# A fused attention and two-mixture kernel: the tile blocks of the first mixture reordered, ranks taken two slots behind the choice, and a fourth output row buffer

## The chip, the core and the metric

The kernel runs on one core of a Trainium2 chip. The metric is the device time of one execution in microseconds (us). Within the core TensorE (PE) multiplies matrices and leaves its results in PSUM banks; VectorE (DVE), ScalarE (ACT) and GpSimd (POOL) work on elements; SyncE (SP) issues most of the DMA transfers. Each engine works through its own list of instructions in order, and waits on semaphores for the others.

## The reference

2176 tokens of 512 numbers come out of a windowed attention with global tokens (4 sequences of 512 local and 32 global tokens, 8 heads). Two mixtures follow:

```python
h = x @ w_in                      # [2176, 512] @ [512, 2048]
g = where(h >= 1, h, where(h <= -1, 0, (h + 1)**2 / 4))
y = g @ w_out                     # [2176, 2048] @ [2048, 512]

logits = (y / |y|) @ (emb / |emb|).T / tau          # 8 experts
idx = argmax(logits, axis=1)
gate = softmax(logits)[arange, idx]
for e in range(8):
    m = idx == e
    out[m] = gate[m] * (relu(y[m] @ w1[e]) @ w2[e])  # 512 -> 1024 -> 512
```

## The kernel before

The tokens make 17 tiles of 128 rows: 16 of local tokens and one of all the global ones. Attention fills the first 155 us or so; the change doesn't touch it. Then one loop (L1361) writes out the order of the work slot by slot. There are 80 slots of the first mixture (5 blocks of tiles, 16 slices f of the 2048 inner columns each), then 40 of the second (5 blocks of its own, 8 slices each), and two more that finish it. A slot is counted below by its f in its block, or from 0 at the start of the second mixture.

In a slot of the first mixture TensorE runs `up1` (L759): twelve matmuls of 128 columns per tile, since each product is made of three with operands split into a high and a low part; the result `hps` has one of two PSUM banks. `act1` (L773) makes `g_` from it (two ScalarE passes `t_`, then VectorE), splits `g_` into `gh` (ScalarE) and later `gl` (`act1b`, L789, VectorE), and splits a slice of `w_out` into `woh` and `wol` (`wout`, L793). `down1` (L804) uses `gh` and `gl` two slots later: three matmuls of 512 columns for each tile, added up in one PSUM bank per tile over the 16 slices. So a block of four tiles has 24 matmuls a slot, and one of three has 12 shorter ones and 9. `sizes` (L623) gives the blocks 4, 2, 4, 4 and 3 tiles; the first two run interleaved, slice by slice. At a block's end `y_out` (L639) copies each tile's rows into a buffer `y` (three in rotation, and for the tiles in `YOB`, L637, one of the output row buffers `ob1` to `ob3`) and stores them to DRAM.

Then each tile must be routed: eight `logits` (L669, one VectorE pass of 512 columns per expert, against the expert's row held in `hTh`, `hTl`, `yTh`, `yTl`, `hb` or `ob0`), the sum of squares `ysq` (L652, ScalarE), `choose` (L677, five small VectorE instructions that end in the one-hot row `ohot`), and `route3` (L690), which ranks each token among those of its expert. `route3` has TensorE multiply `ohot` by a triangle and the running count `acc` by ones, in a PSUM bank of tag T (there are two); VectorE then adds `ohot` to `acc` (L701) and picks out the rank (L703, L707).

This work is spread over the slots of the next block as a list `rq`, one entry a slot, which is popped behind `act1` and ahead of `act1b` and `down1`. On VectorE an entry so stands between `wol` and `gl`, and on TensorE between the up and the down matmuls. `pieces` (L832) plans the list: each item has a cost (1.0 for a logit, 1.2 for `choose`, 0.8 for `route3`), `lim` is what a slot may take (3.5 with five tiles, 2.9 otherwise), and a `None` makes the rest of that tile wait for the next slot. The `None` behind `choose` puts `route3` one slot behind it. The last tiles' list (`pieces_end`, L864) is written out by hand, in six entries, and runs in slots 2 to 7 of the second mixture.

Other work has fixed places. In the third and fourth block x of the next block is loaded at f = 4 (`x_load`, L729) and split at f = 9 and 11 (`x_split`, L741: ScalarE copies the high part `xh`, VectorE subtracts for `xl`, in two pieces for the last block, whose last tile is the global one). At the end of the fourth block `pick` (L881) counts the tokens ranked so far and chooses the most frequent expert, whose weights are read from DRAM; the last block splits them (`es_split`, L1194: a ScalarE and a VectorE pass of 1024 columns each) and transposes the first tiles of the second mixture (`e_tr`, L1205: four matmuls into a bank of tag T, then two times `exh` on ScalarE and `exl` on VectorE). The second mixture multiplies all tiles by that expert (`e_up`, L1213, with `eg` and `el`; `e_down`, L1233), and stores the rows that chose it: `ob` (L1249) is written by VectorE or ScalarE, and an indirect store is issued by POOL. The rows of the other experts are gathered in groups of four lists of 32 (`Quad`, L1127): a gather, a transpose `qt`, matmuls `qo` with weights that SP loads by registers read from the routing result, and a `put` (L1115). `second` (L1266) hangs all this on slots with `hook`; `steps1` to `steps2`, `members`, `norms`, `gates`, `digits` and `gate_list` (L907 to L1045) are the small steps from ranks and logits to lists and gates.

Of the kernel before, what the change touches and what calls it, by code (L numbers as in the profile page):

```python
# [9 lines left out]
F32 = mybir.dt.float32  # L10
# [21 lines left out]
def kernel(  # L32
# [587 lines left out]


    MB = 4
    sizes = [4, 2, 4, 4, 3]  # L623
    esizes = [4, 4, 4, 3, 2]
    assert sum(sizes) == sum(esizes) == NTILE
    blocks = [(sum(sizes[:i]) * P, n) for i, n in enumerate(sizes)]
# [7 lines left out]
    rq = []  # L634


    YOB = {3: 1, 4: 2, 5: 3, 9: 1, 13: 1}  # L637

    def y_out(i, yp):  # L639
        if i in YOB:  # L640
# [11 lines left out]
    def ysq(i, y):  # L652
        jk = mp.tile([P, 2 * P], F32, name="jk", tag="jk")
        nc.scalar.activation(out=jk.bitcast(BF16), in_=y, func=AF.Square, accum_out=ssq[:, i : i + 1])
# [22 lines left out]
    def choose(i, n):  # L677

        ix = mp.tile([P, 3, 8], U32, name="ix", tag="ix")
        for j in range(n):  # L680
            nc.vector.max(out=mxl[:, i + j, :], in_=rawl[:, i + j, :])
            nc.vector.max_index(out=ix[:, j, :], in_max=mxl[:, i + j, :], in_values=rawl[:, i + j, :])
        ixf = mp.tile([P, 3], F32, name="ixf", tag="ixf")
        nc.vector.tensor_copy(out=ixf[:, :n], in_=ix[:, :n, 0])
        nc.vector.tensor_tensor(
            out=ohot[:, i : i + n, :], in0=iota[:, :E].unsqueeze(1).to_broadcast([P, n, E]),
            in1=ixf[:, :n].unsqueeze(2).to_broadcast([P, n, E]), op=ALU.is_equal,
        )
# [115 lines left out]
    def down1(g):  # L804
        bi, f = items[g]
        t0, nt = blocks[bi]
        B_ = bs[bi]
        if f == 0:
            B_.yp = [
                ps.tile([P, DM], F32, name=f"yp{i}", tag="T" if bi == 1 else "y", bufs=2 if bi == 1 else 4)  # L810
                for i in range(nt)
            ]
        (gh, gl, _), (woh, wol) = gq.pop(g), wq.pop(g)
        for i in range(nt):
            cs = slice(i * P, (i + 1) * P)
            for k, (gt, wt) in enumerate(((gh, woh), (gh, wol), (gl, woh))):
                nc.tensor.matmul(  # L817
                    B_.yp[i], lhsT=gt[:, cs], rhs=wt, start=f == 0 and k == 0, stop=f == KF - 1 and k == 2
                )
        if f == KF - 1:  # L820
            B_.y = [y_out(t0 // P + i, B_.yp[i]) for i in range(nt)]
            ty.extend((t0 // P + i, y) for i, y in enumerate(B_.y))
            n = (0, 5, 5, 4, 3)[bi]
            rq.extend({NB - 1: pieces_end}.get(bi, pieces)(*[ty.pop(0) for _ in range(n)]))

    ty = []
# [5 lines left out]
    def pieces(*ty):  # L832

        work = []
        for i, y in ty:
            work += [(1.0, lambda i=i, y=y, e=e: logits(i, y, e, e + 1)) for e in range(E)]
            work += [(0.0, lambda i=i, y=y: ysq(i, y)), (0.0, None)]
            work += [(1.2, lambda i=i: choose(i, 1)), (0.0, None), (0.8, lambda i=i: route3(i, 1))]


        lim = 3.5 if len(ty) == 5 else 2.9
        cost = 0.0
        heads = [list(work[13 * j : 13 * j + 13]) for j in range(len(ty))]
        slots = []
        wait = [0] * len(ty)
        while any(heads):
            now = []
            for j, h in enumerate(heads):
                if not h or wait[j] > len(slots):
                    continue  # L850
                while h and cost + h[0][0] <= lim * (len(slots) + 1) + 0.5:
                    c, f = h.pop(0)
                    if f is None:
                        wait[j] = len(slots) + 1
                        break
                    now.append(f)
                    cost += c
                if h and wait[j] <= len(slots):
                    break
            cost = max(cost, lim * len(slots))  # L860
            slots.append(lambda now=now: [f() for f in now])
        return slots

    def pieces_end(*ty):  # L864

        (ta, ya), (tb, yb), (td, yd) = ty
        return [
            lambda: (logits(ta, ya, 0, 5), ysq(ta, ya)),
            lambda: (logits(ta, ya, 5, 8), choose(ta, 1), logits(tb, yb, 0, 2)),
            lambda: (logits(tb, yb, 2, 7), ysq(tb, yb)),  # L870
            lambda: (route3(ta, 1), logits(tb, yb, 7, 8), choose(tb, 1), logits(td, yd, 0, 3), ysq(td, yd)),
            lambda: (logits(td, yd, 3, 8), choose(td, 1)),
            lambda: (route3(tb, 1), count(route3(td, 1)), steps1()),
        ]


# [356 lines left out]
    def e_down(q, tiles=None):  # L1233
        b, f = divmod(q, KF2)
        t0, nt = eblocks[b][0] // P, eblocks[b][1]
        B_ = eb[b]
        if f == 0:
            B_.yp = [ps.tile([P, DM], F32, name=f"eo{i}", tag="y", bufs=4) for i in range(nt)]
        gh, gl = eq[q]
        wh, wl = [w[:, (f % 2) * DM : (f % 2 + 1) * DM] for w in wA[KD + f // 2]]  # L1240
        for i in range(nt) if tiles is None else tiles:
            cs = slice(i * P, (i + 1) * P)
            for k, (a, w) in enumerate(((gh, wh), (gh, wl), (gl, wh))):
                nc.tensor.matmul(  # L1244
                    B_.yp[i], lhsT=a[:, cs], rhs=w, start=f == 0 and k == 0, stop=f == KF2 - 1 and k == 2
                )
            if f == KF2 - 1:
                t = t0 + i
                ob = rp.tile([P, DM], F32, name="ob", tag=f"ob{1 + t % 3}")  # L1249
                if i % 2:  # L1250
                    nc.scalar.activation(out=ob, in_=B_.yp[i], func=AF.Copy, scale=gt[:, 1, t : t + 1])
                else:
                    nc.vector.tensor_scalar(  # L1253
                        out=ob, in0=B_.yp[i], scalar1=gt[:, 1, t : t + 1], scalar2=None, op0=ALU.mult
                    )
                nc.gpsimd.indirect_dma_start(  # L1256
                    out=outs[t], out_offset=bass.IndirectOffsetOnAxis(ap=ide[:, t : t + 1], axis=0), in_=ob,
                    in_offset=None, bounds_check=NTOK - 1, oob_is_err=False,
                )
# [3 lines left out]
    def hook(q, *fs):  # L1263
        hooks.setdefault(q, []).extend(fs)

    def second():  # L1266

        for c in range(6, NC):
            hook(c - 6, lambda c=c: es_split(c))
        for b in range(1, NEB):  # L1270
            q, nt = KF2 * (b - 1), eblocks[b][1]
            if b > 1:
                hook(q + 1, lambda b=b: e_load(b, 0), lambda b=b: e_load(b, 1))
                q += 3
            for i in range(nt):
                hook(q + i, lambda b=b, i=i: e_tr(b, i))
                if i + 2 < nt:
                    hook(q + i, lambda b=b, i=i: e_load(b, i + 2))
        TE = blocks[NB - 2][0] // P
        hook(-11, lambda: norms(0, TE))  # L1280
        hook(-7, lambda: gates(0, TE))
        hook(-5, lambda: members(0, TE))
        hook(7, steps_e)
        hook(8, steps_e2, lambda: members(TE, NTILE), steps1b)
        hook(9, steps1c, lambda: quads[0].regs(0, NQ4))
        hook(10, steps2, lambda: norms(TE, NTILE))
        quads = [Quad(j) for j in range(NS1)]
        hook(11, quads[0].gather)
        hook(12, lambda: gates(TE, NTILE))
        hook(13, quads[0].trans)  # L1290
        hook(13, lambda: R.update(rl=digits(R["ohhi"], NTILE, NSTEP, gb)))
        hook(14, lambda: R.update(gsl=gate_list(R["rl"])))
        hook(25, lambda: R.update(nst=nc.values_load(R["exi"][0:1, 0, NQ:], min_val=0, max_val=NQ)))
        for n in range(0, NS1 * NSUB, 2):
            (j, s), q = divmod(n, NSUB), 14 + 3 * n // 4
            r = quads[j]
            hook(q - 3, lambda r=r, s=s: (r.load(s), r.load(s + 1)))
            hook(q, lambda r=r, s=s: (r.mm(s), r.mm(s + 1)))
            if s in (KD, 2 * KD):
                hook(q, lambda r=r, s=s: r.htr(s // KD - 1))  # L1300
            if s == KD and j + 1 < NS1:
                hook(q, lambda j=j: quads[j + 1].regs(0, NQ4))
            if s == 2 * KD and j + 1 < NS1:
                hook(q, lambda j=j: quads[j + 1].gather())
            if s == NSUB - 4 and j + 1 < NS1:
                hook(q, lambda j=j: quads[j + 1].trans())
            if s == NSUB - 2:
                hook(q, lambda r=r: r.put())
# [164 lines left out]
```

## Time and profile before

| | |
|---|---|
| Median of 3 runs (lowest, highest) | 778.2 us (777.36, 779.43) |
| The profiled execution, and its span | 777.95 us, 776.2 us |
| Mean granted clock of TensorE | 0.992 of full |
| TensorE, VectorE, ScalarE, GpSimd busy | 96%, 62%, 48%, 18% of the span |

The profile is one execution as recorded on the chip. The span runs from its first to its last instruction, and the profiled execution's own time is 1.75 us longer. Busy time is given for the whole span and for stretches of it; the granted clock is a share of TensorE's full speed. A wait is the idle time of an engine ahead of an instruction, put down to whatever was last to release it. A timeline row gives the start, the length, the engine, the line, the operation, what is written and read, how many instructions are merged in the row, and in brackets the idle time ahead of it with its releaser. Successive VectorE instructions overlap a little, so their starts are closer than their lengths.

### The profile page before, as it was taken

How to read it: one execution, taken by the hardware profiler on the slowest of the kernel's cores; microseconds unless marked ns; L12 is line 12 of the kernel's file. 1: busy time of each engine (PE TensorE's matmuls, PEld its weight loads, DVE VectorE, ACT ScalarE, POOL GpSimd, SP SyncE). 2: the span in 40 equal slices, each digit the busy share in tenths (PEclk: the TensorE clock that was granted, in tenths of full speed). 3: DMA queues.
4: the chain of work that ended last, by engine and by line, in shares of the span. 5: the costliest groups of instructions: out<-in, count | busy, mean ns of one | idle time of the engine just before them, and what ended most of it. 6: DMA issues, size and time to landing. Idle time of an engine off the chain costs nothing.

```text
span 776.2 us, 14130 instructions
## 1 busy us (share of the span) xinstructions
PE 741.5 (96%) x4861; PEld 596.4 (77%) x4861; DVE 484.0 (62%) x1475; ACT 373.0 (48%) x930; POOL 142.1 (18%) x301
## 2 busy tenths in 40 slices
PE   6999898899999999999999999979999999999996
PEld 5777676788888888888888888868878866677765
DVE  5688888487887757777576867887866402211111
ACT  4888888655455565464545555555311212112110
POOL 5676676402111100000000010000004002002011
PEclk9999999999999999999999999999999999999999
DMA  8588886323233522000200004203201777546340
GB/s 186 130 233 232 242 248 148 110 80 108 87 132 113 184 88 82 1 1 0 82 1 0 1 1 161 83 28 106 71 0 69 244 242 285 183 141 215 109 149 25
DMA packets 74653, 89.36 MB, mean 115 GB/s; under 512 B 27488, under 2 KB 45920, under 8 KB 74576
## 3 DMA queue, kind: packets, MB, share of 16 engines
q1 hardware_dynamic: 64176, 78.96, 33.6%
q10 hardware_dynamic: 8720, 4.46, 2.0%
q0 software_dynamic: 1680, 4.98, 1.6%
q8 instruction: 40, 0.66, 0.3%
q14 instruction: 37, 0.30, 0.1%
HBM read 79.77 MB, written 13.65 MB: 120 GB/s over the span
## 4 chain that ended last, share of the span: by engine, by line
issue 62%; PE 6%; DVE 5%; DMA 3%; POOL 2%; ACT 2%; POOLq 0%; ACTq 0%; DVEq 0%
PE hps L768 3%; DMA out<-ob,ide 2%; PE yp L817 2%; POOL out L1256 1%; DVE wf L221 1%; DVE wf L218 1%; DVE wol L801 1%; DVE wf L215 0%; DMA raw<-in_moe_w_in 0%; POOL gt L959 0%; DVE wof L218 0%; PE pv L534 0%; POOL yg L1110 0%; PE pv L545 0%; DVE wof L221 0%
## 5 line engine op out<-in xcount | busy, mean ns | idle before, releaser
L768 PE MATMUL hps<-xh,winh 128*128 128x512 f32 (+2 forms) x320 | 115.2, 360 | 1.7 <-DVE g__2920 L784 1.7
L768 PE MATMUL hps<-xh,winl 128*128 128x512 f32 (+2 forms) x320 | 114.5, 358 | 0.0
L768 PE MATMUL hps<-xl,winh 128*128 128x512 f32 (+2 forms) x320 | 114.4, 358 | 0.0
L817 PE MATMUL yp<-woh,gh 128*128 128x512 f32 x272 | 108.0, 397 | 0.0
L817 PE MATMUL yp<-wol,gh 128*128 128x512 f32 x272 | 106.7, 392 | 0.0
L1228 DVE SCALAR_TENSOR_TENSOR el<-eh,eg 128x512 fp32r<-128x512 f32 (+2 forms) x40 | 24.5, 612 | 117.7 <-ACT eg L1227 117.4
L1227 ACT ACTIVATE eg<-eh 128x512 fp32r<-128x512 f32 (+2 forms) x40 | 21.4, 535 | 99.7 <-PE eh L1222 87.5
L768 PEld LDWEIGHTS hps<-xh,winh 128*128 128x128 f32 x320 | 60.5, 189 | 10.5 <-DVE g__2920 L784 1.9
L768 PEld LDWEIGHTS hps<-xh,winl 128*128 128x128 f32 x320 | 60.4, 189 | 8.5
L768 PEld LDWEIGHTS hps<-xl,winh 128*128 128x128 f32 x320 | 60.4, 189 | 7.5
L1256 POOL DMA_INDIRECT out<-ob,ide x17 | 18.2, 1073 | 230.0 <-DVE ob L1253 224.4
L1222 PE MATMUL eh<-exh,wh 128*128 128x512 f32 (+2 forms) x160 | 59.8, 374 | 0.0
L471 ACT ACTIVATE sm<-sm,st 128x160 f32<-128x160 f32 x128 | 53.4, 425 | 12.5 <-DVE st L461 12.1
L817 PEld LDWEIGHTS yp<-wol,gh 128*128 128x128 f32 x272 | 51.4, 189 | 9.5
L817 PEld LDWEIGHTS yp<-woh,gh 128*128 128x128 f32 x272 | 51.3, 188 | 9.4
L1222 PE MATMUL eh<-exh,wl 128*128 128x512 f32 (+2 forms) x160 | 57.3, 358 | 0.9 <-PEq L1427 0.9
L1222 PE MATMUL eh<-exl,wh 128*128 128x512 f32 (+2 forms) x160 | 57.3, 358 | 0.0
L493 POOL TENSOR_SCALAR pn<-sm,st 128x128 f32<-128x128 f32 x128 | 51.0, 417 | 23.6 <-DVE kw L339 7.0
L1244 PE MATMUL eo<-wh,eg 128*128 128x512 f32 x136 | 53.3, 392 | 0.0
L1244 PE MATMUL eo<-wl,eg 128*128 128x512 f32 x136 | 53.2, 391 | 0.0
L1244 PE MATMUL eo<-wh,el 128*128 128x512 f32 x136 | 53.1, 391 | 0.0
L801 DVE TENSOR_TENSOR wol<-wof,woh 128x512 fp32r<-128x512 f32 x64 | 43.9, 686 | 0.0
(797 smaller groups left out, 1598.0 us busy)
## 6 DMA issues: line engine op xcount, KB each, us to landing
rw<-in_moe_w SPq DMA_DIRECT2D x128, 256.0 KB
raw<-in_moe_w_out SPq DMA_DIRECT2D x12, 512.0 KB
raw<-in_moe_w_in SPq DMA_DIRECT2D x11, 512.0 KB
k<-in_k_l SPq DMA_DIRECT2D x16, 256.0 KB
xsc<-xs ACTq DMA_DIRECT2D x16, 256.0 KB
ysc<-y SPq DMA_DIRECT2D x16, 256.0 KB
rw<-in_moe_w SPq DMA_DIRECT2D x8, 512.0 KB
ye<-ysc SPq DMA_DIRECT2D x16, 256.0 KB
```

The costliest lines, as they stand in the source:

```text
L218: nc.vector.scalar_tensor_tensor(out=du, in0=hi, scalar=0xC0000000, in1=du, op0=ALU.bitwise_and, op1=ALU.bitwise_or)
L221: nc.vector.scalar_tensor_tensor(out=du, in0=lo, scalar=29, in1=du, op0=ALU.logical_shift_right, op1=ALU.bitwise_or)
L471: nc.scalar.activation(out=sm[:, i, :], in_=sm[:, i, :], func=AF.Exp, scale=-1.0, bias=st[:, 0, i : i + 1], accum_out=st[:, 1, i : i + 1],)
L493: eng_of[AT["f4"][i]].tensor_scalar(out=pn[:, i, :].rearrange("p (c x) -> p c x", c=2), in0=sel(sm[:, i, :]), scalar1=st[:, 2, i : i + 1], ...
L768: nc.tensor.matmul(hp_[:, :n], lhsT=wt[:, kk, fs], rhs=xt, start=kk == 0 and i == 0, stop=kk == KD - 1 and i == 2)
L801: nc.vector.tensor_tensor(out=wol, in0=wof[f // 2][:, f % 2, :], in1=woh.bitcast(F32), op=ALU.subtract)
L817: nc.tensor.matmul(B_.yp[i], lhsT=gt[:, cs], rhs=wt, start=f == 0 and k == 0, stop=f == KF - 1 and k == 2)
L1222: nc.tensor.matmul(hps[:, :n], lhsT=w[:, fs], rhs=x, start=kk == 0 and i == 0, stop=kk == KD - 1 and i == 2)
L1227: nc.scalar.activation(out=gh, in_=hps[:, :n], func=AF.Relu)
L1228: nc.vector.scalar_tensor_tensor(out=gl, in0=hps[:, :n], scalar=0.0, in1=gh.bitcast(F32), op0=ALU.max, op1=ALU.subtract)
L1244: nc.tensor.matmul(B_.yp[i], lhsT=a[:, cs], rhs=w, start=f == 0 and k == 0, stop=f == KF2 - 1 and k == 2)
L1256: nc.gpsimd.indirect_dma_start(out=outs[t], out_offset=bass.IndirectOffsetOnAxis(ap=ide[:, t : t + 1], axis=0), in_=ob, in_offset=None, bo ...
```

## The change

The blocks become 4, 2, 4, 3 and 4 tiles. A second `None` puts `route3` two slots behind `choose`; the rates become 3.7 with five tiles and 2.3 otherwise. The last block's four tiles have a list of seven entries, in which the last two tiles are ranked by one call of `route3`. The hooks of the second mixture that depend on the routing, and all of the quads, move by one slot. `ob` gets a fourth buffer, `yTl`, and tile 16 in place of tile 13 has its y in `ob1`.

```diff
-    sizes = [4, 2, 4, 4, 3]
+    sizes = [4, 2, 4, 3, 4]
...
-    YOB = {3: 1, 4: 2, 5: 3, 9: 1, 13: 1}
+    YOB = {3: 1, 4: 2, 5: 3, 9: 1, 16: 1}
...
-            n = (0, 5, 5, 4, 3)[bi]
+            n = (0, 5, 5, 3, 4)[bi]
...
-            work += [(1.2, lambda i=i: choose(i, 1)), (0.0, None), (0.8, lambda i=i: route3(i, 1))]
-
-
-        lim = 3.5 if len(ty) == 5 else 2.9
+            work += [(1.2, lambda i=i: choose(i, 1)), (0.0, None), (0.0, None), (0.8, lambda i=i: route3(i, 1))]
+
+
+        lim = 3.7 if len(ty) == 5 else 2.3
         cost = 0.0
-        heads = [list(work[13 * j : 13 * j + 13]) for j in range(len(ty))]
+        heads = [list(work[14 * j : 14 * j + 14]) for j in range(len(ty))]
...
-        (ta, ya), (tb, yb), (td, yd) = ty
+        (ta, ya), (tb, yb), (tc_, yc), (td, yd) = ty
         return [
-            lambda: (logits(ta, ya, 0, 5), ysq(ta, ya)),
-            lambda: (logits(ta, ya, 5, 8), choose(ta, 1), logits(tb, yb, 0, 2)),
-            lambda: (logits(tb, yb, 2, 7), ysq(tb, yb)),
-            lambda: (route3(ta, 1), logits(tb, yb, 7, 8), choose(tb, 1), logits(td, yd, 0, 3), ysq(td, yd)),
-            lambda: (logits(td, yd, 3, 8), choose(td, 1)),
-            lambda: (route3(tb, 1), count(route3(td, 1)), steps1()),
+            lambda: (logits(ta, ya, 0, 6), ysq(ta, ya)),
+            lambda: (logits(ta, ya, 6, 8), choose(ta, 1), logits(tb, yb, 0, 4), ysq(tb, yb)),
+            lambda: (logits(tb, yb, 4, 8), choose(tb, 1), logits(tc_, yc, 0, 1)),
+            lambda: (route3(ta, 1), logits(tc_, yc, 1, 6), ysq(tc_, yc)),
+            lambda: (route3(tb, 1), logits(tc_, yc, 6, 8), choose(tc_, 1), logits(td, yd, 0, 3)),
+            lambda: (logits(td, yd, 3, 8), choose(td, 1), ysq(td, yd)),
+            lambda: (count(route3(tc_, 2)), steps1()),
         ]
...
-                ob = rp.tile([P, DM], F32, name="ob", tag=f"ob{1 + t % 3}")
+                ob = rp.tile([P, DM], F32, name="ob", tag=("ob1", "ob2", "ob3", "yTl")[t % 4])
...
-        hook(7, steps_e)
-        hook(8, steps_e2, lambda: members(TE, NTILE), steps1b)
-        hook(9, steps1c, lambda: quads[0].regs(0, NQ4))
-        hook(10, steps2, lambda: norms(TE, NTILE))
+        hook(8, steps_e)
+        hook(9, steps_e2, lambda: members(TE, NTILE), steps1b)
+        hook(10, steps1c, lambda: quads[0].regs(0, NQ4))
+        hook(11, steps2, lambda: norms(TE, NTILE))
         quads = [Quad(j) for j in range(NS1)]
-        hook(11, quads[0].gather)
-        hook(12, lambda: gates(TE, NTILE))
-        hook(13, quads[0].trans)
-        hook(13, lambda: R.update(rl=digits(R["ohhi"], NTILE, NSTEP, gb)))
-        hook(14, lambda: R.update(gsl=gate_list(R["rl"])))
-        hook(25, lambda: R.update(nst=nc.values_load(R["exi"][0:1, 0, NQ:], min_val=0, max_val=NQ)))
+        hook(12, quads[0].gather)
+        hook(13, lambda: gates(TE, NTILE))
+        hook(14, quads[0].trans)
+        hook(14, lambda: R.update(rl=digits(R["ohhi"], NTILE, NSTEP, gb)))
+        hook(15, lambda: R.update(gsl=gate_list(R["rl"])))
+        hook(26, lambda: R.update(nst=nc.values_load(R["exi"][0:1, 0, NQ:], min_val=0, max_val=NQ)))
         for n in range(0, NS1 * NSUB, 2):
-            (j, s), q = divmod(n, NSUB), 14 + 3 * n // 4
+            (j, s), q = divmod(n, NSUB), 15 + 3 * n // 4
             r = quads[j]
             hook(q - 3, lambda r=r, s=s: (r.load(s), r.load(s + 1)))
```

## Rows read from the trace of the kernel before

In the tables of stretches the columns are the length, the busy time (with the number of instructions) of PE, PEld (weight loads), DVE, ACT and POOL, the granted clock, the DMA engines' busy share and GB/s.

**Rows 1.** Page, part 1: busy us (share of the span) x instructions.
```profile
PE 741.5 (96%) x4861; PEld 596.4 (77%) x4861; DVE 484.0 (62%) x1475; ACT 373.0 (48%) x930; POOL 142.1 (18%) x301
```

**Rows 2.** Table of stretches: length, then busy us (x instructions) of each engine, granted clock.
```profile
320.00:340.00 20.00, 20.00 (x93) 16.38 (x92) 13.69 (x36) 10.71 (x19) 0.00 (x0) 1.00 0.00 0
...
500.00:520.00 20.00, 15.39 (x85) 13.51 (x83) 17.79 (x59) 11.00 (x23) 0.00 (x0) 1.00 0.18 53
```

**Rows 3.** TensorE's waits from 150 us: us in total, times, longest.
```profile
PE rk L696 <- DVE ohot L685: 4.7, 2, 4.2
...
PE rk L697 <- DVE acc L701: 1.4, 1, 1.4
...
PE qo L1178 <- DVE gsl L991: 1.4, 1, 1.4
```

**Rows 4.** Table of stretches of 2 us, columns as in rows 2.
```profile
520.00:522.00 2.00, 1.95 (x10) 1.59 (x11) 2.00 (x6) 0.00 (x0) 0.00 (x0) 0.72 0.00 0
522.00:524.00 2.00, 2.00 (x7) 1.61 (x6) 0.95 (x3) 1.89 (x4) 0.00 (x0) 0.50 0.00 0
524.00:526.00 2.00, 2.00 (x13) 2.00 (x12) 1.97 (x8) 1.47 (x2) 0.00 (x0) 0.93 0.04 10
```

**Rows 5.** Timeline of VectorE, last block: start, us, instruction.
```profile
516.14 1.22 DVE L1095 TENSOR_TENSOR wl<-rw,wh 128x1024 fp32r<-128x1024 f32 x1
...
519.17 0.17 DVE L681 MAX8 mxl<-rawl 128x8 f32<-128x8 f32 x1
...
519.91 0.69 DVE L672 SCALAR_TENSOR_TENSOR jk<-y,ebchTh 128x512 bf16<-128x512 f32 x1
```

**Rows 6.** Timeline of VectorE, one slot of three tiles.
```profile
472.55 0.56 DVE L784 SCALAR_TENSOR_TENSOR g__5998<-t__5997,hps 128x384 f32<-128x384 f32 x1 [0.67 <-ACT t__5997 L783]
...
473.67 0.69 DVE L672 SCALAR_TENSOR_TENSOR jk<-y,ebchTl 128x512 bf16<-128x512 f32 x1
...
475.50 0.56 DVE L791 TENSOR_TENSOR gl__6000<-g__5998,gh 128x384 fp32r<-128x384 f32 x1
...
476.74 0.56 DVE L784 SCALAR_TENSOR_TENSOR g__6045<-t__6044,hps 128x384 f32<-128x384 f32 x1 [0.68 <-ACT t__6044 L783]
```

**Rows 7.** Timeline of VectorE, fourth block (four tiles).
```profile
398.29 0.69 DVE L784 SCALAR_TENSOR_TENSOR g__5268<-t__5267,hps 128x512 f32<-128x512 f32 x1 [0.97 <-ACT t__5267 L783]
...
403.73 0.69 DVE L784 SCALAR_TENSOR_TENSOR g__5316<-t__5315,hps 128x512 f32<-128x512 f32 x1 [1.58 <-ACT t__5315 L783]
```

**Rows 8.** Timeline of VectorE, split of the next block's x.
```profile
422.41 0.69 DVE L755 TENSOR_TENSOR xl<-xl,xh 128x512 fp32r<-128x512 f32 x1 [0.61 <-ACT xh L753]
```

**Rows 9.** Timeline, last block: VectorE's `gl__6304`, and TensorE's first use of it.
```profile
503.21 0.56 DVE L791 TENSOR_TENSOR gl__6304<-g__6302,gh 128x384 fp32r<-128x384 f32 x1
...
507.37 0.40 PE L817 MATMUL yp<-woh,gl__6304 128*128 128x512 f32 x1
```

**Rows 10.** Timeline, second mixture: VectorE and TensorE about the last two ranks.
```profile
574.98 0.69 DVE L1228 SCALAR_TENSOR_TENSOR el<-eh,eg 128x512 fp32r<-128x512 f32 x1 [0.82 <-ACT eg L1227]
...
575.59 0.15 DVE L701 TENSOR_TENSOR acc<-acc,ohot 128x8 bf16<-128x8 bf16 x1
...
575.79 0.19 PE L697 MATMUL rk<-acc,ones_bf 128*128 128x8 bf16 x2 [1.40 <-DVE acc L701]
...
576.05 0.17 DVE L703 TENSOR_TENSOR rt<-rk,ohot 128x8 f32<-128x8 f32 x1
```

**Rows 11.** Timeline, second mixture: VectorE's second `exl`, TensorE's first quad matmul.
```profile
621.41 0.42 DVE L1106 TENSOR_TENSOR exl<-tt,exh 128x256 fp32r<-128x256 f32 x1 [0.44 <-ACT exh L1105]
...
621.98 1.92 PE L1178 MATMUL qo<-rw,yTh 128*32 128x512 f32 x16 [1.39 <-DVE gsl L991]
```

**Rows 12.** Who waited for tile `ob` (us, times); then POOL's timeline.
```profile
  ACT ob L1251: 9.3, 2
...
759.56 0.98 POOL L1119 DMA_INDIRECT out<-ob,ids  x1 [12.28 <-DVE ob L1118]
...
771.92 0.98 POOL L1256 DMA_INDIRECT out<-ob,ide  x1 [0.31 <-ACT ob L1251]
```

## The prediction

> **What bounds the kernel now.** I began with the busy table of the page: TensorE is busy 96% of the span [rows 1]. Then the table of stretches of 20 us, to see where it is not full: from 160 us to the tail nearly every one has 20.00 us of TensorE work, as 320 to 340 has, and 500 to 520 has 15.39 [rows 2]. TensorE sets the pace, so what counts is why it stands still. Its list of waits from 150 us on gives three that the change touches [rows 3]: 4.7 us for `ohot`, one of them 4.2; 1.4 for `acc`; 1.4 put down to `gsl`. The 4.2 us cost more than themselves: right after them, in the stretches of 2 us from 520, the granted clock is 0.72, 0.50 (the lower of its two levels, 1.2 GHz) and 0.93 [rows 4], which loses (0.28 + 0.50 + 0.07) x 2 = 1.7 us.
>
> Why the 4.2: `choose` of the third tile began on VectorE at 519.17, and its rank matmuls, one slot behind it in TensorE's order, had been due some 4 us earlier [rows 5]. A slot of three tiles takes 4.19 us (472.55 to 476.74, `g__` to `g__`), and VectorE is at work for 3.5 of it with three logits [rows 6]. The last block adds splits of weights (1.22 each [rows 5]) and transposed tiles to that, so VectorE falls behind and the rank waits for it.
>
> **The change, part by part.** The sum is made against the profiled execution: 777.95 us, which is a span of 776.2 and 1.75 around it, and 0.25 under the median of 778.2.
>
> *Blocks of 3 and 4 tiles exchanged.* The same matmuls run in another order, so TensorE's own work stays. The choice of the expert still comes after the ranks of tiles 0 to 8 (the planner has the last of them in slot 14 of the fourth block, before and after) and TE stays 10, so the second mixture has the same expert and the same work. What moves is VectorE's load. The last block now has slots of 5.44 us [rows 7]; in 16 of them, 87 us, VectorE has 16 x 1.83 (`g_`, `wol`, `gl` at 0.61 from start to start), 24 logits x 0.61, three choices and ranks x 1.2, six splits x 1.2 and four transposed tiles x 1.3 (two `exl` of 0.42 with 0.44 between them [rows 11]): 29.3 + 14.6 + 3.6 + 7.2 + 5.2 = 60, and the small instructions of gates and members. No lag is left there.
>
> *The fourth block, now of three tiles, becomes the tight place.* Its slots have 1.60 us of `g_`, `wol` and `gl` (1.12 for the first two, 0.56 less an overlap of 0.08), logits at 0.61 (1.83 for three) [rows 6], a choice at 0.74 (519.17 to 519.91) [rows 5] and a rank at 0.46 (575.59 to 576.05) [rows 10]. Working the planner through by hand at the rate of 3.7 gives for slots 2 to 15: 4.04, 3.43, 4.04, 4.17, 3.43, 4.02, 4.04, 5.99, 3.56, 6.14, 4.02, 3.43, 3.89, 2.34, or 56.5 us against 14 x 4.19 = 58.7. Slots 9 and 11 hold the split of the next block's x: before, 0.61 us of waiting for ScalarE and 0.69 for the columns of two tiles [rows 8]; for three tiles, and 0.42 for the shared one, I take 2.1. VectorE's lag is then 1.8 us after slot 9, 3.1 after 11, 3.0 after 12, 2.2 after 13. How much is free: in the block of three tiles before, `gl__6304` ended at 503.77 and TensorE first used it at 507.37 [rows 9]; of these 3.6 us 0.5 (the shorter wait for `ohot`) and 0.2 (four transposes, 512 columns in all, at 5.44 / 24 per matmul of 512) won't be there, so 2.9, and 2.4 where a slot has four logits instead of two and a choice. The ranks, two slots behind, have a slot more. A lag of 3.1 meets 2.4 to 2.9: I put a stall of 0.5 us there; its ends are 0 and 6 (rival a).
>
> *Ranks two slots behind.* No instruction is added; the extra slot of each list is paid by the rates, and the last rank still comes in the slot where it came before. Removed: 4.7 us of waits and 1.7 of clock [rows 3, 4].
>
> *Seven steps at the end, ranks of the last two tiles in one group.* One more tile's logits, choice and rank move into the second mixture, with slots of about 5.4 us. The fullest of them (six logits, a choice, `el`, a transposed tile) asks 3.7 + 0.7 + 0.6 + 1.3 = 6.3, the next 4.4, so a lag of 1 us is gone one slot later, ahead of any rank that needs it. The group has the eight matmuls of two single ranks, and one product, one reduction and one sum less. Before, the second rank waited 1.40 us for `acc`, whose sum stood behind `el` on VectorE [rows 10]; in the group TensorE adds the first tile's counts itself, and that wait is gone. The last choice stays one slot ahead of its rank, as before, where no wait is listed [rows 3]. Against grouping speaks the Trainium skill, Perfetto Trace Analysis, section Optimizing Scalar/DVE Operations: where VectorE isn't saturated but leaves bubbles on other engines, instructions should be broken up so that work is done sooner. VectorE was idle 0.82 us ahead of that `el` [rows 10]; by the page the group would win nothing, and the sum would be 1.4 smaller. I go by the row, since the wait is for a sum that the group does away with.
>
> *Everything behind it one slot later.* This passes POOL's norms and gather, SP's register and weight loads and TensorE's quads, all by the same slot, so the distances between them stay; the loads of transposed tiles, which stand behind the register loads on SP, keep their slots. The last `put`'s store, issued at 759.56, moves by a slot; the kernel's last one goes at 771.92 [rows 12], so it stays inside. One distance changes. In slot 14 a transposed tile, the gate list and the first quad matmul stood together, and TensorE stood 1.39 us ahead of the quad, until 621.98 [rows 11]. The row names `gsl`, the last thing to end; but there are two banks for such tiles, the gate list had taken one, and the quad got the other, which the transposed tile's second `exl` left only at 621.83. Now that tile is a slot ahead. Removed: 1.4 us (0 if the wait was for `gsl`, which stays where it was).
>
> *A fourth output buffer.* ScalarE waited 9.3 us in two places for a store to land before it could write `ob` [rows 12]; TensorE's waits show none of it [rows 3], being fed two slots ahead. I take 0. `yTl` is last read in slot 7 and first written as `ob` in slot 9. The y tiles 13 and 16 only exchange buffers that are free long before.
>
> **Sum:** 4.7 + 1.7 + 1.4 + 1.4 = 9.2 removed, 0.5 added, 8.7 less: 769.25 for the profiled execution, 769.5 for the median. The ends: 9.2 less and a little of ScalarE's 9.3, about 767, and rival (a)'s 775.
>
> **Rivals.**
> (a) *VectorE becomes the bound of the fourth block.* It is filled to 56.5 of 58.7 us. Behind a late ScalarE copy it lost 0.61 us [rows 8]; lost in each of 14 slots that makes 8.5 more, 6.3 over the supply and 3.8 over what is free: a stall of 4 to 6 us, 773 to 775. For it: slots 9 and 11 ask 6 us each. Against it: with 3.5 us of work a slot of three tiles still left it 0.68 idle [rows 6]. The Trainium skill, Perfetto Trace Analysis, section Identifying the Most-Contended Engine, speaks for it: it judges TensorE by its weight loads and VectorE by occupancy, which from 500 to 520 are 13.5 and 17.8 us [rows 2], so that by the page VectorE bounds such a block. By the waits it held TensorE up at ranks alone. Chance 0.2.
> (b) *The wait only moves.* A slot more doesn't cure the last block's lag; waits for `gl` take the place of those for `ohot`, and only the 2.8 us in the second mixture are won: 775.4. Against it: 60 of 87 us. Chance 0.08.
> (c) *Slower.* In the two slots with the x split VectorE is held so long by ScalarE's copies, which stand behind `gh` and `ysq`, that TensorE stalls 4.2 us twice and loses 1.7 us of clock each time: 11.8 against 9.2, 780.8. It decides once that stage costs VectorE some 13 us more than tallied, and these copies were waited for 0.61 us [rows 8]. Chance 0.05.
> (d) *No change:* stalls of about 9 us in all stay or return elsewhere, 777 to 779. Chance 0.07.
>
> **The numbers.** The forecast has 0.6, and 767 to 771.5 for itself. 0.3%, 2.3 us, is about what a measurement of this kernel can tell from no change: faster than 775.9 takes the forecast, (a) and (b), 0.88; within it (d), 0.07; slower (c), 0.05. The range, 766.9 to 775.5, takes in (a), (b) and the ends.
>
> **What would show it.** Right: no wait for `ohot` above 0.3 us, none for `acc` or `gsl`; a granted clock of 1.00 from 160 us to the tail; VectorE nearly full in the fourth block, with at most 1 us of waits for `gl` in its slots 11 to 14; no ScalarE wait for a store ahead of `ob`. Wrong: TensorE waits of over 2 us or a clock under 1.00 in the fourth block, or a new wait of quads or gathers in the second mixture.

## The result, and the profile after

The changed kernel takes 769.78 us (median of four runs, 767.39 to 771.02) beside 778.5 for the kernel before on the same chip: a ratio of 0.9885, 95% interval 0.9856 to 0.9914. The forecast was 769.5. The profiled execution took 769.06 us, of which 767.4 are its span.

The page's busy table first, then the table of stretches of the fourth block (360 to 440 us, now of three tiles) and the last one, with the columns of [rows 2]:

```profile
PE 741.1 (97%) x4861; PEld 596.6 (78%) x4861; DVE 483.1 (63%) x1472; ACT 372.3 (49%) x930; POOL 139.9 (18%) x301
```

```profile
380.00:400.00 20.00, 20.00 (x102) 18.11 (x101) 18.13 (x50) 11.52 (x23) 0.00 (x0) 1.00 0.21 68
400.00:420.00 20.00, 20.00 (x107) 17.71 (x106) 17.94 (x58) 12.10 (x25) 0.00 (x0) 1.00 0.00 0
420.00:440.00 20.00, 20.00 (x107) 17.41 (x106) 17.61 (x54) 11.13 (x24) 2.10 (x1) 1.00 0.01 1
...
500.00:520.00 20.00, 20.00 (x95) 16.39 (x94) 16.79 (x41) 12.51 (x23) 0.00 (x0) 1.00 0.20 66
```

TensorE's busy time is what it was [rows 1]; the 500 to 520 that had 15.39 us of it [rows 2] has 20.00, at a clock of 1.00. VectorE is now fullest in the fourth block, 17.6 to 18.1 of 20. TensorE's waits from 150 us to the tail are these two, both there before (1.7 and 0.9 us):

```profile
PE hps L768 <- DVE g__2920 L784: 1.7, 1, 1.7
PE eh L1223 <- PEq L1428: 0.7, 1, 0.7
```

All three of [rows 3] are gone. To see where the time came from I cut each profiled execution at two marks: the first up matmul, and the last down matmul of the first mixture. In the view of a tile these are the first start of `hps` (148.1 us before, 149.2 after) and the last start of `yp`; this is the latter's row of the changed kernel:

```profile
L817 PE MATMUL yp<-wol,gh x272: 387/389/401, 159.8 to 536.5; 128*128 128x512 f32 x136
```

| us | ahead of the first mixture | first mixture | from there to the end |
|---|---|---|---|
| before | 148.1 | 394.0 | 234.1 |
| after | 149.2 | 387.3 | 230.9 |
| after, a second profile | 150.9 | 387.3 | 231.3 |

So the first mixture gives 6.7 us and the second about 3. The first column, attention, which the change doesn't touch, lies anywhere from 146.4 to 150.9 in the profiles of this study. I therefore compare kernels below by the other two columns, each read from one profile.

In the fourth block VectorE goes like this (start, length, instruction, and in brackets the idle time ahead of it):

```profile
410.49 0.56 DVE L784 SCALAR_TENSOR_TENSOR g__5445<-t__5444,hps 128x384 f32<-128x384 f32 x1
...
412.36 0.96 DVE L755 TENSOR_TENSOR xl<-xl,xh 128x768 fp32r<-128x768 f32 x1 [0.67 <-ACT xh L753]
413.24 0.42 DVE L755 TENSOR_TENSOR xl<-xg,xh 128x256 fp32r<-128x256 f32 x1
...
416.34 0.55 DVE L784 SCALAR_TENSOR_TENSOR g__5503<-t__5502,hps 128x384 f32<-128x384 f32 x1
...
419.84 0.54 DVE L784 SCALAR_TENSOR_TENSOR g__5548<-t__5547,hps 128x384 f32<-128x384 f32 x1
...
425.36 0.55 DVE L791 TENSOR_TENSOR gl__5550<-g__5548,gh 128x384 fp32r<-128x384 f32 x1
426.65 0.56 DVE L784 SCALAR_TENSOR_TENSOR g__5597<-t__5596,hps 128x384 f32<-128x384 f32 x1 [0.73 <-ACT t__5596 L783]
...
430.07 0.55 DVE L791 TENSOR_TENSOR gl__5599<-g__5597,gh 128x384 fp32r<-128x384 f32 x1
```

and TensorE first uses the last two results here:

```profile
426.65 0.40 PE L817 MATMUL yp<-woh,gl__5550 128*128 128x512 f32 x1
...
431.05 0.39 PE L817 MATMUL yp<-woh,gl__5599 128*128 128x512 f32 x1
```

From `g__` to `g__`, slot 9 took VectorE 5.85 us; slot 11 took 6.07 (419.84 to the end of its `gl` at 425.91). Its results were ready 0.74 and 0.43 us before use: VectorE only just keeps up.

In the second mixture, the last choice and the group of two ranks, VectorE and then TensorE:

```profile
574.10 0.17 DVE L685 TENSOR_TENSOR ohot<-iota,ixf 128x8 bf16<-128x8 f32 x1
575.09 0.69 DVE L1229 SCALAR_TENSOR_TENSOR el<-eh,eg 128x512 fp32r<-128x512 f32 x1 [0.82 <-ACT eg L1228]
575.69 0.17 DVE L703 TENSOR_TENSOR rt<-rk,ohot 128x16 f32<-128x16 f32 x1
```

```profile
574.20 0.18 PE L696 MATMUL rk<-ohot,tri_bf 128*128 128x8 bf16 x1
...
574.31 0.17 PE L696 MATMUL rk<-ohot,tri_bf 128*128 128x8 bf16 x1
```

Both ranks run ahead of `el`, with no sum on VectorE between them as in [rows 10]; but the last choice ended at 574.27, 0.04 us before its matmul. There is nothing to spare here. The first quad matmul, the last row below, starts 4.6 us after the transposed tile's second `exl` has left its bank (614.19), and 0.11 us before the instruction that writes `gsl`:

```profile
613.77 0.42 DVE L1107 TENSOR_TENSOR exl<-tt,exh 128x256 fp32r<-128x256 f32 x1 [0.44 <-ACT exh L1106]
...
618.93 0.22 DVE L992 TENSOR_REDUCE gsl<-gi 128x19 f32<-128x57 f32 x1 [1.84 <-PE gi L922]
```

```profile
618.82 1.92 PE L1179 MATMUL qo<-rw,yTh 128*32 128x512 f32 x16
```

And ScalarE's writes of `ob`, from the view of that tile (the instruction, and what its idle time ahead of them ended with), have no store among their releasers, unlike [rows 12]:

```profile
L1252 ACT ACTIVATE ob<-eo,gt x8: 687/687/689, 581.6 to 762.1; 128x512 f32<-128x512 f32 x8
...
  PE eo L1245: 9.0, 8
```

### The profile page after: what moved, and what is told of

Its sections match the earlier page's. It is cut to its first block, busy times and chain, and to the rows that moved or that the text cites. A ratio compares the mean times of both kernels' runs of the same rounds, so it can differ in the third digit from the quotient of the medians.

```text
span 767.4 us, 14112 instructions
## 1 busy us (share of the span) xinstructions
PE 741.1 (97%) x4861; PEld 596.6 (78%) x4861; DVE 483.1 (63%) x1472; ACT 372.3 (49%) x930; POOL 139.9 (18%) x301
## 4 chain that ended last, share of the span: by engine, by line
PE 58%; issue 17%; DMA 3%; POOL 1%; ACT 0%; POOLq 0%; DVE 0%; ACTq 0%
PE yp L817 24%; PE hps L768 24%; PE eh L1223 4%; PE eo L1245 4%; DMA out<-ob,ide 3%; POOL out L1257 1%; PE tt L1103 1%; PE pv L534 0%; POOL yg L1111 0%; PE pv L545 0%; POOLq L1470 0%; POOL out L1120 0%; DVE exl L1107 0%; PE rk L697 0%; POOLq L1294 0%
```

## The experiments

All edits but the last are to the changed kernel. Times are medians, beside 778.36, 778.92 and 779.73 us for the kernel before in the three groups of runs. "First" and "second" are the two columns above (387.3 and 231 in the changed kernel).

| | us | ratio to before, interval | first | second |
|---|---|---|---|---|
| changed kernel again | 770.19 | 0.9877 (0.9857 to 0.9896) | 387.3 | 231.3 |
| one slot of distance | 770.63 | 0.9895 (0.9875 to 0.9915) | 389.1 | 231.0 |
| old blocks | 771.37 | 0.9901 (0.9880 to 0.9923) | 390.4 | 230.9 |
| more VectorE work | 773.69 | 0.9935 (0.9912 to 0.9959) | 392.3 | 231.2 |
| single ranks | 770.86 | 0.9896 (0.9879 to 0.9913) | 389.0 | 232.3 |
| ranks in pairs | 769.20 | 0.9878 (0.9860 to 0.9897) | 387.0 | 231.4 |
| quads back | 769.74 | 0.9893 (0.9876 to 0.9911) | 387.4 | 232.2 |
| three buffers | 771.86 | 0.9915 (0.9897 to 0.9932) | 387.4 | 232.9 |
| three buffers, quads back | 770.51 | 0.9896 (0.9866 to 0.9926) | 387.4 | 232.6 |
| before with a fourth buffer | 778.04 | 0.9990 (0.9971 to 1.0010) | 394.0 | 233.8 |

Most of these differ from the changed kernel by less than the intervals can tell. The waits and the two columns decide. Between the two profiles of the changed kernel, and between the kernel before and its copy with a fourth buffer, the listed waits of over 1 us repeat within 0.1 us and the two columns within 0.4. The first column has an exception, a low clock at its start, which is named where it occurs.

**The changed kernel again**, on the chip of the first group.

> The changed kernel once more, as the yardstick of this call: 8 to 10 us faster than the kernel before, no wait of TensorE over 1 us from 160 us to the tail.

Measured: 770.19 us, no wait but the two shown above, the second of 1.0 us here. So 1.0 instead of 0.7 is no effect of an edit.

**One slot of distance**: the exchanged blocks with the rank one slot behind its choice.

```diff
-            work += [(1.2, lambda i=i: choose(i, 1)), (0.0, None), (0.0, None), (0.8, lambda i=i: route3(i, 1))]
+            work += [(1.2, lambda i=i: choose(i, 1)), (0.0, None), (0.8, lambda i=i: route3(i, 1))]
...
-        heads = [list(work[14 * j : 14 * j + 14]) for j in range(len(ty))]
+        heads = [list(work[13 * j : 13 * j + 13]) for j in range(len(ty))]
```

> The changed kernel with the planned ranks one slot behind the choice again (rates 3.7 and 2.3 kept). Theory, both parts are needed: with three tiles the fourth block leaves VectorE a lag of 1 to 2.5 us, and at one slot's distance a choice without any lag ends only about 1 us before its rank is due, so TensorE waits for `ohot` there twice, about 0.6 and 1.3 us, 1.5 to 3 us in all, with no dip of the clock: 1.5 to 3 us slower than the changed kernel. Rival, the exchange of the blocks is the cure by itself: no wait for `ohot`, same time as the changed kernel within 0.3 us.

Measured: two waits, together 1.4 us, and a first mixture of 389.1.

```profile
PE rk L696 <- DVE ohot L685: 1.4, 2, 1.0
```

The exchange without the second slot of distance (and with the new rates, which no run varies alone) brings 394.0 - 389.1 = 4.9 of the 6.7 us; no stretch between 160 us and the tail shows a lowered clock, so that cost went with the long wait.

**Old blocks**: 4, 2, 4, 4 and 3 tiles with everything else as changed (the end list without the fourth tile, an empty entry ahead of the group, the old rate of 2.9, and the tile counts and y buffers that go with the old blocks).

```diff
-    sizes = [4, 2, 4, 3, 4]
+    sizes = [4, 2, 4, 4, 3]
...
-        lim = 3.7 if len(ty) == 5 else 2.3
+        lim = 3.7 if len(ty) == 5 else 2.9
...
-            lambda: (count(route3(tc_, 2)), steps1()),
+            lambda: None,
+            lambda: (count(route3(tb, 2)), steps1()),
```

> The changed kernel with the old blocks of 4, 2, 4, 4, 3 tiles (four tiles' ranks planned at 2.9 in the last block, three tiles' list at the end with ranks at least two slots behind but for the last, same hooks). Theory: the ranks no longer wait, but the last block is still overfilled for VectorE, whose lag of some 4.6 us about slots 11 to 13 passes the 2.9 us that `gl` allows: TensorE waits 1 to 3 us in all for `gl`, without a dip of the clock, 1 to 3 us slower than the changed kernel. Rival A, distance alone cures it: no wait, same time. Rival B, the wait only moves: 4 us or more for `gl` and a dip of the clock, 5 to 6 us slower than the changed kernel.

Measured: 390.4. The waits for `ohot` are gone here too, and the clock stays at 1.00, but the last block now stands behind VectorE itself (waits from 505 to 530 us, TensorE's, PE, and its weight loads', PEld):

```profile
PEld hps L768 <- DVE g__6479 L784: 1.0, 1, 1.0
PEld hps L768 <- DVE g__6533 L784: 0.9, 1, 0.9
...
PEld yp L817 <- DVE gl__6535 L791: 0.6, 1, 0.6
PE hps L768 <- DVE g__6479 L784: 0.5, 1, 0.5
PE hps L768 <- DVE g__6533 L784: 0.5, 1, 0.5
```

TensorE's own list shows 1.0 us, at the PSUM bank of `hps` that `g_` must free, which I had not named. The weight loads' list is worth reading beside it: several short waits there lengthen the slots without a TensorE wait of their own (slots of 5.07, 5.24 and 5.40 us at the end of the block, against 4.2 to 4.5). So the distance without the exchange brings 3.6 of the 6.7 us. The exchange's 4.9 and this 3.6 overlap: each cures the long wait, and only both leave nothing.

**More VectorE work**: one more logit pass, a repeat of one that the list has, in each of 14 slots of the fourth block.

```diff
+            if ty[0][0] == 5 and len(slots) < 14:
+                now.append(lambda i=ty[0][0], y=ty[0][1]: logits(i, y, 0, 1))
             slots.append(lambda now=now: [f() for f in now])
```

> The changed kernel with one more logit pass (0.61 us of VectorE) in each of 14 slots of the fourth block; it repeats a logit already there, so the output stays. Theory: the fourth block is at VectorE's edge, 55 to 56.5 of 59 us filled and 0.4 to 0.7 us of lag free at slots 11 and 12; 8.5 us more lead to waits for `gl` or `g_` of 4 to 6 us in all: 774 to 776 us. Rival, VectorE has room there, since TensorE showed no wait: under 1.5 us slower than the changed kernel.

Measured: 392.3, 5.0 more; 1.6 of it lie in one slot at the start, at 157 us, where the clock was 0.87 (150 to 160 us) and not 1.00 in this execution (that slot took 7.19 us and not 5.58, and the single ranks below show it too; the edit isn't there). The other 3.4 are in the fourth block:

```profile
PE yp L817 <- DVE gl__5568 L791: 2.0, 1, 2.0
...
PE yp L817 <- DVE gl__5461 L791: 0.6, 1, 0.6
```

```profile
400.00:420.00 20.00, 20.00 (x108) 17.68 (x106) 19.05 (x58) 10.71 (x23) 0.00 (x0) 1.00 0.00 1
420.00:440.00 20.00, 17.41 (x92) 14.95 (x92) 19.01 (x61) 9.87 (x20) 0.00 (x0) 1.00 0.00 1
```

Some 14 x 0.61 = 8.5 us of work cost 3.4, under the 4 expected. This is rival (a) made true: VectorE at 19 of 20, the waits at `gl`. A wait of 2.0 us left the clock at 1.00.

**Single ranks** for the last two tiles, in the same entry.

```diff
-            lambda: (count(route3(tc_, 2)), steps1()),
+            lambda: (route3(tc_, 1), count(route3(td, 1)), steps1()),
```

> The changed kernel with the last two tiles ranked by two single calls, as before, in the same slot. Theory: the second waits for the sum `acc`, which stands behind `el` on VectorE: a wait of 1.3 to 1.6 us at the rank, 1.4 us slower than the changed kernel. Rival (finer pieces are as good): wait under 0.3 us, same time.

Measured: the old wait is back, and the second column is 1.0 to 1.4 longer, as expected. Of the 1.7 us more in the first, 1.6 lie in its first full slot (7.15 us and not 5.58), where the clock is low (0.83 from 150 to 160 us); the edit isn't there. Below are the wait, and a row of the table of stretches.

```profile
PE rk L697 <- DVE acc L701: 1.4, 1, 1.4
```

```profile
150.00:160.00 10.00, 8.27 (x53) 6.67 (x53) 3.22 (x6) 4.07 (x8) 0.00 (x0) 0.83 0.17 49
```

**Ranks in pairs**: two tiles per `route3` in the planned lists too.

```diff
-            nc.vector.tensor_tensor(out=acc, in0=acc, in1=ohot[:, i, :], op=ALU.add)
+            for j in range(n):
+                nc.vector.tensor_tensor(out=acc, in0=acc, in1=ohot[:, i + j, :], op=ALU.add)
```

> The changed kernel with the planned ranks taken in groups of two tiles where there are two, five groups fewer. Theory: a slot with a rank group takes TensorE 0.2 to 0.26 us more than one without (5.65 to 5.70 against 5.44), for the change of matmul kind and not for the work, so five fewer save 1.0 to 1.3 us of TensorE time: 768.5 us. Rival: the 0.22 us follows the number of rank matmuls, which stays 8 for a pair: no gain.

Measured: 387.0, so 0.3 us gained, and a time within the interval of the changed kernel's. A pair lengthens a slot of TensorE by 0.28 to 0.36 us, a single rank by 0.20 to 0.26: a pair saves some 0.1 to 0.2, not what I had expected, and five of them about 0.7. The other 0.4 went in one slot of the fourth block (423.27 to 427.85, 4.58 us and not 4.18), where no wait of TensorE is listed but one of its weight loads is:

```profile
PEld yp L818 <- DVE gl__5540 L792: 0.6, 1, 0.6
```

The pairs leave no rank in slot 12, which fits: without it TensorE comes for `gl` earlier. The changed kernel is that close to the stall that the prediction had there.

**Quads back**: gather to quads one slot earlier again.

```diff
-        hook(14, quads[0].trans)
+        hook(13, quads[0].trans)
...
-        hook(15, lambda: R.update(gsl=gate_list(R["rl"])))
+        hook(14, lambda: R.update(gsl=gate_list(R["rl"])))
...
-            (j, s), q = divmod(n, NSUB), 15 + 3 * n // 4
+            (j, s), q = divmod(n, NSUB), 14 + 3 * n // 4
```

> The changed kernel with the quads, their gather, gates and gate list one slot earlier, so that transposed tile, gate list and first quad matmul share slot 14 again. Theory (the PSUM bank of the transposed tile): a wait of 1.2 to 1.5 us ahead of the first quad matmul comes back, 1.4 us slower than the changed kernel. Rival (the wait had another cause and went for another reason, such as the order of the loads): no wait.

Measured: the wait is back, and the second column is 0.9 to 1.3 longer. The median doesn't show it.

```profile
PE qo L1179 <- DVE gsl L992: 1.4, 1, 1.4
```

**Three buffers** for `ob`, as before.

```diff
-                ob = rp.tile([P, DM], F32, name="ob", tag=("ob1", "ob2", "ob3", "yTl")[t % 4])
+                ob = rp.tile([P, DM], F32, name="ob", tag=f"ob{1 + t % 3}")
```

> The changed kernel with three buffers for `ob` as before. Theory: ScalarE waits 9 us in two places for stores again, TensorE feels at most 0.4 us of it: same time as the changed kernel within 0.4 us. Rival, the fourth buffer has part of the gain: 1 us or more slower.

Measured: a second column of 232.9, 1.6 to 2.0 longer, and a wait of TensorE that neither kernel has. ScalarE's row and TensorE's, from the timeline:

```profile
638.54 0.69 ACT L1252 ACTIVATE ob<-eo,gt 128x512 f32<-128x512 f32 x1 [5.98 <-DMA out<-ob,ide]
```

```profile
639.28 0.50 PE L1245 MATMUL eo<-wh,eg 128*128 128x512 f32 x1 [1.33 <-ACT ob L1252]
```

ScalarE stood 5.98 us for a store to land, and TensorE in turn for the bank of `eo` that ScalarE had not read. I had taken 0 for this buffer, so two more runs ask where its worth comes from.

**Three buffers, quads back**: both edits above at once.

> The changed kernel with three output buffers and with the quads and their steps one slot earlier again. Theory A: the 1.3 us that three buffers cost comes from the one-slot move, which puts the stores of the second group of rows beside other loads, so that one lands 6.0 us after ScalarE wants its buffer. Then TensorE waits 0.4 us or less for ob here, the 1.4 us wait of the first quad matmul for a PSUM bank is back, and the time is that of the kernel with the quads back alone, about 769.7 us. Theory B: three buffers cost 1.3 us wherever the quads stand; then both waits are there and the time is near 771.

Measured: TensorE doesn't wait for `ob`, and its 1.4 us wait at the quad is there (theory A).

```profile
PE qo L1179 <- DVE gsl L992: 1.4, 1, 1.4
```

```profile
ACT ob L1252 <- PE qt L1155: 3.1, 1, 3.1
```

With the quads in their old slots the second group's row waits 3.1 us in place of 5.98, and TensorE bears that. The wait is put down to a quad's transpose, which this instruction doesn't read; it needs the bank of `eo` and a free buffer, so I take it for the same store. That store was issued on POOL at 632.83 with three buffers alone, and ScalarE wrote at 638.54, 5.71 us later; with the quads back it was issued at 633.45 and ScalarE wrote at 636.30, after 2.85. These are the two stretches, in this order (the DMA share is the last column but one):

```profile
632.83:638.54 5.71, 5.12 (x23) 3.92 (x21) 0.47 (x1) 0.00 (x0) 2.99 (x3) 1.00 0.98 343
633.45:636.30 2.85, 2.85 (x23) 1.11 (x22) 0.47 (x1) 0.00 (x0) 2.24 (x3) 1.00 0.33 99
```

So the store that landed late went out while the DMA engines were 0.98 busy, the other at 0.33. That fits theory A, the neighbouring loads; no run varies those loads by themselves.

**Before with a fourth buffer**: the edit of `ob` alone, in the kernel before.

> The kernel before with the fourth output buffer alone. Prediction's step: it is worth 0 to 0.4 us there, 778.0 to 778.5 us, with the waits for ohot (4.7 us), acc (1.4) and gsl (1.4) as they were, and no ScalarE wait for a store ahead of ob. Rival: the buffer is worth 1.3 us by itself, 777.

Measured: ratio 0.9990, not to be told from no change. ScalarE's waits for stores are gone, and TensorE's are those of before:

```profile
PE rk L696 <- DVE ohot L685: 4.7, 2, 4.2
...
PE rk L697 <- DVE acc L701: 1.4, 1, 1.4
PE qo L1178 <- DVE gsl L991: 1.4, 1, 1.4
```

## Why the prediction was right

The sum was 8.7 us; the two columns fell by 9.5 to 9.9, and the medians by 8.7 here and 8.2 in the second comparison. That 769.5 meets 769.78 so closely is in part luck: the stages that the change touches gave 0.8 to 1.2 us more than the sum, and in the profiles compared the stage ahead of them took 1.1 us longer. Point by point:

*The `ohot` waits and the clock, 4.7 + 1.7.* Right: 394.0 to 387.3 is 6.7. As predicted no rank waits, and the clock is 1.00 from 160 us to the tail. The long wait causes the low clock as far as the runs show: in the kernel before with a fourth buffer both repeat, and where an edit takes the wait away the dip goes too. What made VectorE late in the kernel before was more than the splits and transposed tiles that the prediction names: from 504.82 to 507.58, in the last block, it ran the small instructions of `gates`, 2.8 us, and only then its next `g_`.

*The fourth block as the tight place.* The mechanism is right, the 0.5 us stall is not there. VectorE's slots came out as planned: 5.85 for 5.99, 6.07 for 6.14, and the x split from 411.69, where VectorE fell idle, to 413.66, or 1.97 for 2.1; over slots 9 to 12 it was 0.3 us quicker than the tally. What failed is what this load was set against, in three places.

First, the supply: I let TensorE run 4.19 us in every slot. A slot with a rank takes longer, as its starts of `up1` show (398.38 to 402.79 holds a rank, the next slot none):

```profile
398.38 0.33 PE L768 MATMUL hps<-xh,winh 128*128 128x384 f32 x1
...
402.79 0.34 PE L768 MATMUL hps<-xh,winh 128*128 128x384 f32 x1
...
406.95 0.33 PE L768 MATMUL hps<-xh,winh 128*128 128x384 f32 x1
```

4.41 against 4.16: each rank gives VectorE some 0.2 us. Between slot 9, which VectorE began without a lag, and the tightest use, at 431.05, lie the ranks of slots 9, 12 and 14, 0.6 us in all.

Second, the room of 2.9 us. In the changed kernel `g__5445` of slot 9 starts 3.54 us after its slot's first up matmul (406.95 to 410.49). The slot of [rows 9], from which the room was read, is not like that. VectorE stood idle there and `g_` came 4.99 us after the first up matmul, some 1.4 later (TensorE and VectorE, kernel before):

```profile
495.14 0.42 PE L768 MATMUL hps<-xh,winh 128*128 128x384 f32 x1
```

```profile
500.13 0.56 DVE L784 SCALAR_TENSOR_TENSOR g__6302<-t__6301,hps 128x384 f32<-128x384 f32 x1 [0.62 <-ACT t__6301 L783]
```

That makes the room 1.4 us too small. On the other side the way from that matmul to the use at 507.37, 12.23 us, was 1.3 longer than the same way without ranks, waits and transposes (385.82 to 396.77 in the changed kernel), and I took off only 0.7. By my estimate the room, ranks left out, was really some 0.8 us larger.

Third, and against VectorE: 0.73 us of idle time ahead of `g__5597` (the row above), which no term has. It waited for ScalarE's `t__5596`. TensorE had finished the up matmuls for it at about 422, but ScalarE's `ysq` stood ahead, and waited for the scratch buffer `jk` that it shares with VectorE's logits:

```profile
424.87 0.63 ACT L654 ACTIVATE jk<-y 128x512 bf16<-128x512 f32 x1 [2.89 <-DVE jk L672]
...
425.50 0.56 ACT L782 ACTIVATE t__5596<-hps,half 128x384 f32<-128x384 f32 x1
```

The second profile of the changed kernel has the same two waits, 2.89 and 0.73. Together 0.3 + 0.6 + 0.8 - 0.7 = 1.0 us, which turns the stall of 0.5 into a spare of about the 0.43 measured. That the term was only 0.5 off is luck: larger errors nearly cancelled. A buffer of its own for `ysq` was not tried.

*Rival (a)* is therefore near: it needs only a little more work in that block. It was priced at 4 to 6 us for 8.5 us of lost time; the run shows 3.4. The Trainium skill, Perfetto Trace Analysis, section Identifying the Most-Contended Engine, judges VectorE by occupancy, and TensorE by the busy share of its weight loads beside its share of peak arithmetic. By occupancy and weight loads alone VectorE would be the bound, if barely, already in the changed kernel: 18.13 of 20 us against 18.11, 17.94 against 17.71, 17.61 against 17.41. No TensorE wait bears that out there; at 19.0 it does.

*Rivals (b) and (c)* fell: no wait for `gl` is listed, and the x split held VectorE for 0.7 us of waiting in each of its two slots, not for 13 us more. (b)'s mechanism is what the old blocks show, with 3.1 us and at `hps` more than at `gl`.

*Ranks of the last two tiles, 1.4.* Right, by the single ranks. The Trainium skill, Perfetto Trace Analysis, section Optimizing Scalar/DVE Operations, says that breaking instructions up may let work be completed sooner where VectorE isn't saturated but leaves bubbles on other engines. Here the trace shows the opposite: taken singly, the ranks wait 1.4 us again, since the wait is for a sum that grouping leaves to TensorE. "One slot ahead of its rank" was closer than I said: 0.04 us.

*The bank at the first quad, 1.4.* Right, and the reading of [rows 11] too: in the changed kernel the quad starts before `gsl` is written, so `gsl` cannot be what it waits for.

*The fourth buffer, 0.* This step failed in its reason. Alone it is worth nothing, as I said; but I priced it in the old order. With the quads moved, three buffers cost 1.6 to 2.0 us, more than the 1.4 that the move wins. The sum is right since the change makes both edits: they are one term, 1.3 to 1.7 for the pair (a second column of 232.6 without both, 230.9 and 231.3 with them), and the move by itself is worth about nothing (232.9).

## What to carry to other kernels

A wait between two engines has two cures, more distance and less load on the late one; each alone left 1.8 to 3.1 us here, and one sees the rest only in the waits that come next, the weight loads' among them. Edits that are worth nothing alone (a buffer) can be what lets another one pay, so price them in the new order, where the stores have moved beside other work. When a pipelined engine is nearly full, count the supply slot by slot: small matmuls on the fast engine are time given to the slow one. Read what is free from a slot in which no engine was already late, and look at what the third engine waits for: here a shared scratch buffer made ScalarE late, and VectorE with it.

## What the runs showed that I had not expected

The stage ahead of the first mixture ends anywhere from 146.4 to 150.9 us in kernels that share it to the letter, which is wider than most effects studied here; the stages behind it repeat within 0.4 us in the profiles that can be compared. The clock in the first slots of the mixture, behind the 1.7 us wait for `g__2920` that all of them have, was 1.00 in most profiles but 0.83 and 0.87 in two, which costs 1.6 us; no edit explains it. And the four rank matmuls of one tile, of eight columns each, lengthen a slot of TensorE by 0.20 to 0.26 us.
